# Attention on clusters and a gated feed-forward block: loads of one pair behind a transpose, logits later and in other banks, the last product stored in halves

## The chip, the cores and the metric

The kernel runs on one core of a Trainium2 chip. The metric is the device time of one execution in microseconds (us). The kernel before took 321.58 us (median of three runs, 321.5 to 322.22).

The core's engines run side by side and each works through its own instructions in order: TensorE (PE in the profile; its weight loads are PEld), VectorE (DVE), ScalarE (ACT), GpSimd (POOL) and SyncE (SP), which here issues nearly all DMAs. A DMA is issued by an engine and then carried out by the core's 16 DMA engines. Matrix products land in PSUM, which has eight banks; everything else lies in SBUF.

## The reference

Four batches, eight heads, 768 tokens, 64 numbers a head. Each query and key goes to the nearest of 16 centroids of its head; a query sees the keys of its own cluster alone. The attention's output, 512 numbers a token, goes through a gated feed-forward block with 1,536 inner columns.

```python
q_assign = argmax(einsum('bhsd,hcd->bhsc', q_n, c_n))      # and k_assign alike
mask = q_assign[:, :, :, None] == k_assign[:, :, None, :]
scores = where(mask, scale * q @ k.T, -1e9)
x = (softmax(scores) @ v).transpose(0, 2, 1, 3).reshape(B * S, H * D)
out = (sigmoid(x @ w_gate) * (x @ w_val)) @ w_out
```

## The kernel before

**Attention.** Heads go in pairs: batch b, pair p, head e of the pair (0 or 1). A step of the main loop is one score product `sc` (line 894): 128 keys against 384 queries of one head, an exponential on ScalarE (line 899), and, two steps later, three products `av` with the values (line 917). There are 96 steps a batch, 384 in all. Batch 1 begins with step 96, batch 2 with step 192, batch 3 with step 288; in them a pair's first use is 24 steps after the one before it (batch 2: steps 192, 216, 240, 264). The last pair of a batch is worked in two halves.

**Preparing a pair** (`pair_prep`, from line 1452) is done long before its first use, with these steps, each under a name:

- `ld`: SyncE loads k, q and v of the pair, 384 KB each (line 212), into three buffers a kind.
- `sp`: VectorE casts to 16 bits and GpSimd makes the remainder (lines 1459 and 1460), giving `hl`.
- `tn0`, `tn1`: SyncE transposes `hl` of head 0 and head 1 by DMA into `T` (`turn`, line 411).
- `lg0`, `lg1`: TensorE makes the logits of a head, 12 small products from `T` into one PSUM bank `lg` (`logits1`, line 435).
- `pk0`, `pk1`: VectorE reduces the logits, finds the maximum and writes the marks `oh` (lines 450, 461, 463, 470). The bank of `lg` is free after the first of these five operations.
- `ot`: SyncE transposes the marks by DMA (line 1477), and `hp0`, `hp1` copy them, four DMAs called hops, into rows of `T` (line 491). The pair's scores need them.
- `vc`, `vs`: casts and sums of v.

After the last step of a pair its outputs are normalised (lines 371 to 376) and SyncE transposes them into `xTb` (line 948), the input of the feed-forward block.

**Feed-forward.** A block of 384 tokens is cut in 12 times two pieces, `g` (line 531, tanh on ScalarE) and `v` (line 547, combined on VectorE into `hT`, line 552), and then output products. In batch 0 these are plain: an output tile `o` of 12 products in one bank (line 685), then a copy (lines 693 and 695). From batch 1 on they are factored in seven products over two output banks (line 822, additions on VectorE, line 769); between `begin` and `end2` the flag `taken["pair"]` says that a product holds both banks. The pieces go one by one between the steps, by a budget of nanoseconds a step (`ns...`). The last block is closed by `closing` (line 576), whose last product, `last`, is made in two halves of 128 columns, `o_end`.

**PSUM.** Four banks are a ring (`bank`, line 162) for scores, `g`, `v` and most other things; two hold `av`; two are output banks (`out_bank`, line 167). `turns` (line 171) takes an output bank, or one of the ring while `taken["pair"]` is set. A tile that takes a bank waits until the former tile of that bank has been read.

**Order.** Nothing is reordered by a tool: the order of the instructions on each engine is that in which the code issues them. `SCHED` says when: a key `b2ld` or `b2p1lg0` is a distance in steps from the pair's first use. The key without a pair (`b2...`) holds for batches 2 and 3, one with `b2p1` for pair 1 of batch 2 alone. The loads stand at first use + `b2ld` + an offset of their own for k, q and v (`b2p1lk` and so on). Within a step the order is: score, what is due at the half step, feed-forward pieces, `av`, what is due at the full step (`run_bg`). An issue on SyncE waits for its data, and what stands behind it waits too.

Of the kernel before, what the change touches and what calls it, by code (L numbers as in the profile page):

```python
# [8 lines left out]
FP = mybir.dt.float32  # L9
# [86 lines left out]
}  # L96


# [1 line left out]
def kernel(  # L100
# [12 lines left out]
    PE, ACT, DVE, POOL, SP = nc.tensor, nc.scalar, nc.vector, nc.gpsimd, nc.sync  # L113
    B, H, S, D = q.shape
    NCL = centroids.shape[1]
    DM = out.shape[1]
# [45 lines left out]
    def bank(n=512, dt=FP, name="bank"):  # L162
        return ring.tile([128, n], dt, tag="ring", name=name)
# [3 lines left out]
    def out_bank():  # L167
        taken["op"] += 1
        return op.tile([128, DM], FP, tag="o", name="o")
# [94 lines left out]
    HF, HD = NFC // 2, DM // 2  # L264
# [163 lines left out]
    def logits(t, h, n, copy=None):  # L428
        return logits1([(t, c, h) for c in range(n)], copy)

    def logits1(groups, copy=None):
        n = len(groups)
        lg = (turns if SCHED.get("lgo1", 0) else bank)(512, FP, name="lg")
        for i, (t, c, h) in enumerate(groups):
            PE.matmul(  # L435
                out=lg[:, bass.ts(i, 32)], lhsT=t[:, c, :],
                rhs=cm[:, h].rearrange("p s n -> p (s n)"), start=True, stop=True,
            )
        lv = lg[:, 0 : n * 32].rearrange("p (c s n) -> p c s n", s=2, n=NCL)
        if SCHED.get("lgr", 0) and (n > 6 or SCHED.get("lgs", 0)):  # L440
            return lv, None
        lo = smp.tile([128, 12, NCL], FP, name="lglo")
        (copy or ACT.copy)(lo[:, 0:n], lv[:, :, 1, :])
        return lv[:, :, 0, :], lo[:, 0:n]
# [53 lines left out]
    def tok(b, t, f):  # L498
        return HB[b, t // 3][:, HF * f : HF * f + HF, bass.ts(t % 3, 128)]

    def store(src, b, c0, n, m=slice(0, DM)):
        def f():
            SP.dma_start(
                out=out[b * S : (b + 1) * S].rearrange("(p c) m -> p c m", c=NCH)[
                    :, c0 : c0 + n, m
                ],
                in_=src,
            )

        d_ = SCHED.get("sd", 0)  # L510
        if d_ > 0 and b < B - 2:
            at(step_no[0] + d_, f)
        else:
            f()
# [61 lines left out]
    def closing(b, gv, ma, mb):  # L576

        ac, order = [], []  # L580
        plus = lambda dst, a, z: DVE.tensor_tensor(dst, a, z, ALU.add)

        def pair(m, bk):
            st = {}
            lhs = {
                1: lambda: tok(b, m.t1, 0), 2: lambda: tok(b, m.t1, 1), 4: lambda: tok(b, m.t2, 1),
                6: lambda: m.of[2], 5: lambda: m.of[1], 7: lambda: m.of[3], 3: lambda: m.of[4],
            }
            rhs = {1: B11, 2: B21, 3: B22, 4: T4, 5: T1, 6: T2, 7: T3}
            C = lambda i, j: st["ob"][:, i, HD * j : HD * j + HD]  # L590

            def mm(o, k, g, n, start, a=0, z=HD):
                w = lhs[k]()
                for c in range(g, g + n):
                    PE.matmul(  # L595
                        out=o, lhsT=w[:, c, :], rhs=rhs[k][:, c, a:z],
                        start=start and c == 0, stop=c == HF - 1, skip_group_check=True,
                    )

            def product(k, g=0, n=HF):  # L600
                def f():
                    z = {1: "a", 4: "d", 6: "x", 7: "x", 5: "y", 3: "y"}[k]
                    if g == 0 and k in (1, 4, 6, 5):
                        if k == 1:
                            st["ob"] = osp.tile([128, 2, DM], FP, name="ob")
                        st[z] = bk(z)
                    o = st[z][:, 0:HD]
                    mm(o, k, g, n, k not in (7, 3))
                    if g + n < HF:
                        return  # L610
                    if k == 1:
                        ACT.activation(C(0, 0), o, AF.Copy)
                    elif k == 4:
                        plus(C(1, 0), o, C(0, 0))
                    elif k == 6:
                        plus(C(0, 1), o, C(0, 0))
                    elif k == 5:
                        plus(C(1, 1), o, C(0, 0))
                    elif k == 7:
                        plus(C(1, 0), o, C(1, 0))  # L620
                        plus(C(1, 1), o, C(1, 1))
                        store(st["ob"][:, 1:2], b, m.t2, 1)
                    else:
                        plus(C(0, 1), o, C(0, 1))
                        store(st["ob"][:, 0:1, HD:DM], b, m.t1, 1, slice(HD, DM))

                return f

            def last(parts):
                def f():  # L630
                    for a, z in parts:
                        o = bank(z - a, name="o_end")
                        mm(o, 2, 0, HF, True, a, z)
                        plus(st["ob"][:, 0, a:z], o, st["ob"][:, 0, a:z])
                    store(st["ob"][:, 0:1, 0:HD], b, m.t1, 1, slice(0, HD))

                return f

            return product, last

        two = {}

        def bank_a(z):
            if z in "ad":
                need(*(("wo", i) for i in range(WOP)), *(("wt", i, c) for i in range(4) for c in range(2)))
                two[z] = out_bank()
            return two[{"x": "a", "y": "d"}.get(z, z)]

        pa, la = pair(ma, bank_a)
        pb, lb = pair(mb, lambda z: bank(512, name="o_end"))  # L650
        early = [pa(k, g, HF // 2) for k in (1, 4, 6, 5) for g in (0, HF // 2)]

        def drained(f):
            def g():
                while aside:
                    aside.pop(0)[1]()
                f()

            return g

        early[0] = drained(early[0])
        atoms = gv[:14]
        for i, x in enumerate(gv[14:]):
            atoms.append(x)
            if i < len(early):
                atoms.append((0.0, early[i]))
        for f in (
            pa(7), pb(1), pb(4), pa(3), pb(6), pb(5), la([(0, HD)]), pb(7), pb(3),
            lb([(0, HD // 2), (HD // 2, HD)]),
        ):  # L670
            atoms.append((0.0, f))
        return atoms
# [278 lines left out]
    step_no = [-4]  # L951

    def at(i, f):
        bg.setdefault(max(i, step_no[0] - 0.5), []).append(f)
# [11 lines left out]
    def need(*names):  # L966
        for n in names:
            assert n in done, n
# [133 lines left out]
    def first(p, e, parts=1):  # L1102
# [55 lines left out]
        def lg(part=0):  # L1158
            cs = [c for s in range(2 if part == 0 else 1) for c in range(*rng(s, part))]
            gs = [(T[0, h], c, h) for c in cs]  # L1160
            if SCHED.get(f"hL{h}", 0) and h:
                st["lg", part] = join(*logits1(gs, SCHED.get(f"hM{h}", 0) and DVE.tensor_copy))
            else:
                st["lg", part] = logits2(gs, h == 0 and part == 0)
# [65 lines left out]
    def rest(p, i):  # L1230
# [41 lines left out]
        def lg(eng=None):  # L1272
            gs = [(T[0, 2 * p + e], 6 + P0 + c, 2 * p + e) for e in range(2) for c in range(N)]
            st["lg"] = join(*logits1(gs)) if SCHED.get(f"rL{p}" + "_" * (i - 1), 0) else logits2(gs)
# [25 lines left out]
        def pl(e, eng=None):  # L1300
            if SCHED.get(RO, 0):
# [10 lines left out]
               lg=-15, pk=-14, ot=-10, pl0=-9, pl1=-7, oe=-9, hp=-8)  # L1312
# [17 lines left out]
    a = P[0, 0, 0]  # L1330
# [53 lines left out]
    def put(nm, key, u, off, f, arg):  # L1384
# [15 lines left out]
        def go():  # L1400
# [7 lines left out]
                 lg=-9, pk=-8, ot=-5, pl0=-4, pl1=-3)  # L1408
# [121 lines left out]
    for b in range(B):  # L1530
        xT = xtp.tile([128, NDC, S], HP, tag="xTb", name="xTb")
        key = min(b, 1)
        for i in range(2 if b else NPT):
# [4 lines left out]
            c0, cn = PARTS[i] if b == 0 else (3 * i, 3)  # L1538
            for w in range(1 + (cn > 3)):
                z = cn // (1 + (cn > 3))  # L1540
# [51 lines left out]
```

## Time and profile before

| | |
|---|---|
| median of three runs | 321.58 us |
| profiled execution, its own time | 323.41 us |
| its span, first to last instruction | 321.6 us |
| TensorE busy | 314.1 us (98%), 3510 matmuls |
| VectorE, ScalarE, GpSimd busy | 225.2, 230.8, 108.9 us |
| DMA | 45.16 MB, 140 GB/s over the span |
| the chain that ended last | TensorE 92%, VectorE 3%, DMA 2% |
| granted TensorE clock | 1.000 |

The profiled execution is one execution with the hardware profiler on; its times are microseconds from the span's start. A row of the order of time has start, length, engine, line, operation, what it writes and reads, sizes, and in brackets the idle time of the engine before it with what ended it. Matmuls are pipelined, and the profile's ends of matmuls are modelled: two that follow each other without a wait overlap. So a loss on TensorE is read from start to start where it is short. For a DMA the length is that of the issue on SyncE; the time from issue to landing is told by the view of DMA issues.

### The profile page before, as it was taken

Reading aid. Unit: us, or ns where it says so; the run is one execution under the profiler, and the core shown is the slowest. Engines: PE = TensorE matmul, PEld = TensorE weight load, DVE = VectorE, ACT = ScalarE, POOL = GpSimd, SP = SyncE. Lnnn points to the kernel's source line nnn. Section 1 sums busy time; section 2 is a strip of 40 time slices with the busy share of each in tenths; the row PEclk is TensorE's granted clock in tenths of the full one; section 3 lists DMA queues with packets and bytes.
Section 4 is the critical chain, followed back from the end, with each engine's and each line's share of the span. In section 5 each row is a group of like instructions: output and inputs, shape, how many; then the busy total and the mean of one; then the engine's idle time right before and its main releaser. Section 6 shows DMA issues by size and latency. Waiting matters only on the chain.

```text
span 321.6 us, 9181 instructions
## 1 busy us (share of the span) xinstructions
PE 314.1 (98%) x3510; PEld 222.1 (69%) x3510; DVE 225.2 (70%) x598; ACT 230.8 (72%) x521; POOL 108.9 (34%) x145
## 2 busy tenths in 40 slices
PE   7999999999999998999999999999999999999996
PEld 5888666766766665666777678666777678667775
DVE  5899656777787676686778678775766456456666
ACT  6688988787889986877767786887877875332320
POOL 6887464154435364423233342524102011000000
DMA  7999996748776996965665545952512122200103
GB/s 204 372 264 193 237 169 122 190 93 237 236 114 184 166 218 142 275 175 108 111 200 138 188 101 155 258 89 53 110 27 66 39 27 73 84 2 1 65 2 131
DMA packets 77708, 45.16 MB, mean 140 GB/s; under 512 B 56864, under 2 KB 75104, under 8 KB 77664
## 3 DMA queue, kind: packets, MB, share of 16 engines
q1 hardware_dynamic: 73696, 39.73, 49.4%
q0 software_dynamic: 3680, 4.72, 8.8%
q8 instruction: 27, 0.44, 0.6%
q14 instruction: 17, 0.14, 0.2%
q10 hardware_dynamic: 288, 0.13, 0.1%
HBM read 28.34 MB, written 6.29 MB: 108 GB/s over the span
## 4 chain that ended last, share of the span: by engine, by line
PE 92%; DVE 3%; DMA 2%; ACT 1%; issue 0%; ACTq 0%; POOL 0%; DVEq 0%
PE g L531 20%; PE v L547 19%; PE sc L894 18%; PE av L917 10%; PE o L822 10%; PE o L685 3%; DMA T<-hl 2%; PE lg L435 2%; PE o_end L595 2%; PE lg L422 1%; PE o L595 1%; PE oh_ps L1203 1%; PE t_ps L1143 1%; PE wm L985 1%; PE t_ps L1026 0%
## 5 line engine op out<-in xcount | busy, mean ns | idle before, releaser
L899 ACT ACTIVATE es<-sc 128x384 f16<-128x384 f32 x384 | 173.9, 492 | 40.5 <-PE sc L894 29.9
L894 PE MATMUL sc<-T 128*128 128x384 f16 x384 | 117.5, 326 | 0.4 <-DVE T L1224 0.4
L917 PEld LDWEIGHTS <-es 128*128 128x128 f16 x1152 | 81.3, 98 | 35.1 <-ACT es L899 0.2
L917 PE MATMUL av<-va,es 128*128 128x65 f16 x1152 | 97.6, 194 | 0.0
L552 DVE SCALAR_TENSOR_TENSOR hT<-th,v 128x384 f16<-128x384 f32 x96 | 53.1, 553 | 57.3 <-PE av L917 36.4
L531 PE MATMUL g<-xTb,wg 128*128 128x384 f16 x384 | 78.0, 326 | 0.2 <-DVE hT L552 0.2
L547 PE MATMUL v<-xTb,wv 128*128 128x384 f16 x384 | 78.1, 326 | 0.1
L537 ACT ACTIVATE th<-g 128x384 f32<-128x384 f32 x96 | 47.2, 492 | 34.7 <-PE g L531 15.6
L376 POOL TENSOR_TENSOR xp<-t,rec 128x384 f16<-128x384 f32 (+1 forms) x30 | 21.6, 721 | 98.0 <-DVE rec L373 50.3
L531 PEld LDWEIGHTS <-wg 128*128 128x128 f16 x384 | 37.3, 97 | 19.2 <-issue 0.4
L547 PEld LDWEIGHTS <-wv 128*128 128x128 f16 x384 | 37.4, 98 | 19.0 <-issue 0.3
L894 PEld LDWEIGHTS <-T 128*128 128x128 f16 x384 | 37.1, 97 | 0.6 <-DVE T L1224 0.5
L1460 POOL TENSOR_TENSOR hl<-kraw,hl 128x384 f16<-128x384 f32 x22 | 20.3, 922 | 41.4 <-DVE hl L1459 26.7
L1460 POOL TENSOR_TENSOR hl<-qraw,hl 128x384 f16<-128x384 f32 x22 | 21.2, 963 | 11.1 <-DVE hl L1459 11.1
L769 DVE TENSOR_TENSOR ob<-o,ob 128x256 f32<-128x256 f32 (+1 forms) x35 | 17.9, 523 | 6.9 <-PE o L822 4.1
L685 PE MATMUL o<-wo,hT 128*128 128x512 f16 x72 | 19.9, 379 | 0.0
L371 DVE TENSOR_TENSOR t<-av,sv 128x390 f32<-128x390 f32 (+1 forms) x30 | 14.4, 480 | 7.7 <-PE av L917 5.6
L822 PE MATMUL o<-wo,hT 128*128 128x256 f16 x126 | 19.7, 272 | 0.0
L822 PEld LDWEIGHTS <-sum 128*128 128x128 f16 x168 | 16.3, 97 | 4.4
L450 DVE TENSOR_REDUCE lgs<-lg 128x192 f32<-128x384 f32 x23 | 12.7, 551 | 3.7 <-PE lg L435 3.6
L822 PEld LDWEIGHTS <-hT 128*128 128x128 f16 x126 | 12.1, 97 | 3.3
L323 POOL CAST va<-vraw 128x768 f16<-128x768 f32 x15 | 13.0, 866 | 2.3 <-DMA vraw<-in_v_dram 2.3
(158 smaller groups left out, 340.0 us busy)
## 6 DMA issues: line engine op xcount, KB each, us to landing
vraw<-in_v_dram SPq DMA_DIRECT2D x15, 384.0 KB, 5.2
kraw<-in_k_dram SPq DMA_DIRECT2D x14, 384.0 KB, 4.4
qraw<-in_q_dram SPq DMA_DIRECT2D x12, 384.0 KB, 4.3
out_dram<-ob SPq DMA_DIRECT2D x18, 256.0 KB, 2.2
wg<-in_moe_w_gate_dram POOLq DMA_DIRECT2D x2, 768.0 KB, 9.2
wv<-in_moe_w_val_dram POOLq DMA_DIRECT2D x2, 768.0 KB, 10.2
wo<-in_moe_w_out_dram POOLq DMA_DIRECT2D x2, 768.0 KB, 9.0
T<-ohT SPq DMA_DIRECT2D x44, 24.0 KB, 1.9
```

The costliest lines, as they stand in the source:

```text
L376: (eng or POOL).tensor_tensor(x, t[:, 0:nq, 0:64], bcast(rec[:, 0:nq], 64), ALU.mult)
L531: PE.matmul(out=g[:, 0:n], lhsT=wg[fc // WQ][:, dc, fc % WQ, :], rhs=xT[:, dc, t0 : t0 + n], start=(dc == 0), stop=(dc == NDC - 1),)
L537: ACT.activation(th[:, 0:n], g[:, 0:n], AF.Tanh)
L547: PE.matmul(out=w[:, 0:n], lhsT=wv[fc // WQ][:, dc, fc % WQ, :], rhs=xT[:, dc, t0 : t0 + n], start=(dc == 0), stop=(dc == NDC - 1),)
L552: DVE.scalar_tensor_tensor(HB[b, blk][:, fc, 0:n], st[0][:, 0:n], 1.0, w[:, 0:n], ALU.add, ALU.mult)
L685: PE.matmul(out=o, lhsT=HB[b, blk][:, fc, bass.ts(t, 128)], rhs=wo[fc // WON][:, fc % WON, :], start=(fc == 0), stop=(fc == NFC - 1),)
L769: plus = lambda dst, a, z: DVE.tensor_tensor(dst, a, z, ALU.add)
L822: PE.matmul(out=st[z][:, e], lhsT=a[:, c, :], rhs=rhs[:, c, :], start=start and c + e == 0, stop=c == HF - 1, skip_group_check=True,)
L894: PE.matmul(out=sc.rearrange("p (c t) -> p c t", t=128), lhsT=s["k"], rhs=s["q"], start=True, stop=True,)
L899: ACT.activation(es, sc, AF.Exp, scale=SCALE)
L917: PE.matmul(out=av[:, a0 + s["c0"] + i, :], lhsT=s["es"][:, bass.ts(i, 128)], rhs=VA[b, p][:, e, s["j"], :], start=(first and i == 0 and a ...
L1460: POOL.tensor_tensor(hl[:, :, 64:128], r, hl[:, :, 0:64], ALU.subtract)
```

## The change

- `b2p2lk`, `b2p2lq`, `b2p2lv`: the loads of pair 2 of batch 2 move from steps 157, 157.5 and 158.5 to steps 168, 168 and 169. Pair 1's `tn0` stands at step 166.5. (The offsets are set for batch 2 alone; pair 3 of both batches and pair 1 of batch 2 had such offsets already.)
- `b2p1lg0`, `b2p1pk0`: batch 2, pair 1: the logits of head 0 move from step 177 to 180, their marks from step 177 to 180.5.
- `b2pk1`: in all pairs of batches 2 and 3 the marks of head 1 come one step earlier, half a step behind their logits.
- `logits1` takes its bank by `turns` from step 101 on, not from the ring.
- `store` takes an engine, and `last` stores each half of the last product behind its addition: the first half from SyncE, the second from ScalarE, where both went in one store from SyncE. The `last` of the other tile of that block, with one part, stores from SyncE as before.

```diff
-    "b2tn1": -39.5, "b2lg1": -29, "b2pk1": -27.5, "b2ot": -21.0, "b2hp0": -13.5, "b2hp1":
+    "b2tn1": -39.5, "b2lg1": -29, "b2pk1": -28.5, "b2ot": -21.0, "b2hp0": -13.5, "b2hp1":
...
-    "b3p0vs": -30, "b3p0vu": -28, "b3p0vt": -9, "b3p1lg0": -32, "b3p1pk0": -32, "END": 0,
+    "b3p0vs": -30, "b3p0vu": -28, "b3p0vt": -9, "b3p1lg0": -32, "b3p1pk0": -32, "b2p2lk": 10.5, "b2p2lq": 10.5, "b2p2lv": 11.5, "b2p1lg0": -36, "b2p1pk0": -35.5, "END": 0,
...
     def logits1(groups, copy=None):
         n = len(groups)
-        lg = (turns if SCHED.get("lgo1", 0) else bank)(512, FP, name="lg")
+        lg = (turns if step_no[0] > 100 else bank)(512, FP, name="lg")
...
-    def store(src, b, c0, n, m=slice(0, DM)):
+    def store(src, b, c0, n, m=slice(0, DM), eng=SP):
         def f():
-            SP.dma_start(
+            eng.dma_start(
...
             def last(parts):
                 def f():
-                    for a, z in parts:
+                    for i, (a, z) in enumerate(parts):
                         o = bank(z - a, name="o_end")
                         mm(o, 2, 0, HF, True, a, z)
                         plus(st["ob"][:, 0, a:z], o, st["ob"][:, 0, a:z])
-                    store(st["ob"][:, 0:1, 0:HD], b, m.t1, 1, slice(0, HD))
+                        store(st["ob"][:, 0:1, a:z], b, m.t1, 1, slice(a, z), (SP, ACT)[i])
```

## The prediction

> **What bounds the kernel now.** I read the page first, then the busy time of each engine in stretches, then the order of time around the holes.
>
> ```profile
> span 321.6 us, 9181 instructions
> ...
> core 0: us, PE busy (x) PEld busy (x) DVE busy (x) ACT busy (x) POOL busy (x), PEclk, DMA share, GB/s
> 40.00:120.00 80.00, 80.00 (x929) 53.29 (x928) 58.55 (x153) 69.42 (x160) 35.56 (x41) 1.00 0.78 173
> 120.00:123.00 3.00, 1.71 (x27) 1.04 (x24) 1.60 (x5) 1.08 (x3) 1.34 (x2) 1.00 1.12 150
> 123.00:218.00 95.00, 94.93 (x1050) 66.67 (x1049) 70.46 (x186) 73.81 (x166) 33.98 (x41) 1.00 0.67 160
> 218.00:220.00 2.00, 1.79 (x20) 1.07 (x18) 1.46 (x4) 1.19 (x4) 0.00 (x0) 1.00 0.50 114
> 220.00:318.60 98.60, 98.55 (x899) 70.16 (x897) 61.05 (x145) 53.61 (x118) 9.53 (x13) 1.00 0.19 48
> 318.60:321.60 3.00, 0.00 (x0) 0.00 (x0) 0.29 (x1) 0.00 (x0) 0.00 (x0) 1.00 0.48 175
> ```
>
> Each row of a stretch has its length and then the busy time of each engine. From 40 us on TensorE is never idle but in three places: 1.29 us in 120 to 123, 0.21 in 218 to 220, and the 3.0 us after its last matmul. The change adds or removes no matmul, so it can only win there, or lose by opening new holes. The granted clock is 1.00 throughout.
>
> ```profile
> 120.52 0.26 PE L917 MATMUL av<-va,es 128*128 128x65 f16 x3
> 122.06 0.47 PE L435 MATMUL lg<-cm,T 128*128 128x32 f16 x12 [1.29 <-DMA T<-hl]
> ...
> 217.00 0.26 PE L917 MATMUL av<-va,es 128*128 128x65 f16 x3
> 217.09 0.45 PE L435 MATMUL lg<-cm,T 128*128 128x32 f16 x12
> ```
>
> Idle time is measured from a modelled end. From start to start, the logits of 122.06 stand 1.54 us behind the products in front of them; those of 217.09, which wait for nothing, stand 0.09 behind theirs. So that stop costs 1.45. By the count of score matmuls it lies in step 177: it is `lg0` of batch 2's pair 1, one of the two entries that the change moves on their own.
>
> **Part 1: the loads of batch 2's pair 2 go behind pair 1's transpose, pair 1's `lg0` three steps later.** SyncE's issues in order of time (start, length of the issue), then from the view of DMA issues, by windows that hold one each, what four of them took from issue to landing (the first is that of 114.93, then 116.88, 122.14, 126.25):
>
> ```profile
> 112.21 0.58 SPq L212 DMA_DIRECT2D kraw<-in_k_dram  x1
> 112.84 0.46 SPq L212 DMA_DIRECT2D qraw<-in_q_dram  x1
> 114.06 0.37 SPq L212 DMA_DIRECT2D vraw<-in_v_dram  x1
> 114.93 1.86 SPq L411 DMA_TRANSPOSE T<-hl  x1
> 116.88 2.23 SPq L1477 DMA_TRANSPOSE ohT<-oh  x1
> ...
> 122.14 1.46 SPq L411 DMA_TRANSPOSE T<-hl  x1
> 123.71 2.50 SPq L491 DMA_DIRECT2D T<-ohT  x4
> 126.25 1.25 SPq L948 DMA_TRANSPOSE xTb<-xp  x1
> ...
> T<-hl SPq DMA_TRANSPOSE x1, 7.1
> ...
> ohT<-oh SPq DMA_TRANSPOSE x1, 5.7
> ...
> T<-hl SPq DMA_TRANSPOSE x1, 3.5
> ...
> xTb<-xp SPq DMA_TRANSPOSE x1, 2.4
> ...
> 114.00 0.91 POOL L1460 TENSOR_TENSOR hl<-qraw,hl 128x384 f16<-128x384 f32 x1
> ...
> DMA  8999999999200799999999999500000000799999
> q8 instruction: 1, 0.02, 1.3%
> ```
>
> The three loads of 112.21 to 114.06 are the ones moved (planned at steps 157 to 158.5, now 168 to 169). The transpose `tn0` of 114.93 (step 166.5) took 7.1 us behind them and landed at 114.93 + 7.1 = 122.0, just when the logits started; its twin of 122.14, with no loads ahead, took 3.5. Its source was ready at 114.00 + 0.91 = 114.9, so it is issued no earlier than now. Without the loads ahead it lands at 114.93 + 3.5 = 118.4. Step 177 without a stop comes at 120.6, so the landing alone removes the whole 1.45, and `lg0` at step 180 only adds margin (step 192's score stands at 129.68 below: 15 steps in 7.6 us, so 1.5 us for three). The moved loads keep their use: the first cast of that pair's k stands at 125.19, some 123.7 after the change; the issue goes to about 116.9, and behind a transpose, with the 5.7 us that one such took, it lands at 122.6.
>
> The last two rows show 117.0 to 122.5 in 40 slices of 0.1375 us: from 120.5 to 121.7 the DMA engines move nearly nothing, and one 16 KB block of instructions was fetched in this stretch. Some 1.1 us of the 7.1 are this hole. The Trainium skill (Runtime: NRT & Kernel Launch, "Instruction fetch mechanics") says that a 16 KiB refill is mostly hidden; by that rule the hole would be an accident of this execution, which is what rival B takes it for.
>
> What pays for it: `ohT` (116.88) now stands behind the three loads. Their issues take 0.58 + 0.46 + 0.37, with gaps about 1.6 us, so it is issued at 118.5; with the 5.7 us that it took behind the transpose it lands at 124.2 instead of 122.6. The four hops that read it were issued from 123.71 and go to 124.25; `xTb` behind them goes from 126.25 to 126.8. Who needs that:
>
> ```profile
> 129.68 0.33 PE L894 MATMUL sc<-T 128*128 128x384 f16 x1
> 129.84 0.33 PE L531 MATMUL g<-xTb,wg 128*128 128x384 f16 x1
> ...
> 124.41 0.38 PE L685 MATMUL o<-wo,hT 128*128 128x512 f16 x1
> ...
> 124.11 0.69 DVE L693 COPY ob<-o 128x512 f32<-128x512 f32 x1
> ```
>
> Batch 1's first `g` at 129.84 reads that `xTb`. 1.45 earlier it wants it at 128.4. SyncE's issues from 122.14 on stand back to back (each starts 0.04 to 0.1 after the one before ends) and don't move forward: landing 126.25 + 2.4 = 128.65 as it is, 129.2 with the late hops. So 0.25 to 0.8 of the 1.45 goes to this new wait; I take 0.45, nearer the end in which `ohT` lands a little late, since loads and hops overlap in part. The first hops are needed by the score at 129.68, then 128.2; issued at 124.25 they would have to take 4 us to be late.
>
> One more wait hides below it. The plain output that begins at 124.41 now finds the logits in one output bank and must take the bank whose copy runs until 124.11 + 0.69 = 124.80, 0.39 behind its own start. The moved logits, though, stand between the two outputs and take about 0.3 (12 matmuls, 0.45 with the last one's own length), so about 0.1 is left; it comes before `g` and counts inside the 0.45. Net of part 1: -1.45 + 0.45 = **-1.0** (bounds -1.2, and -0.1 in rival B).
>
> **Part 2: logits in the output banks.** From step 101 on `logits1` takes one of two output banks unless a factored product holds both. By the order of products in the trace it does so for 13 of 19 logits; the other six stay in the ring.
>
> ```profile
> 218.55 0.33 PE L894 MATMUL sc<-T 128*128 128x384 f16 x1
> 219.08 0.65 PE L531 MATMUL g<-xTb,wg 128*128 128x384 f16 x3 [0.20 <-DVE hT L552]
> ...
> 218.47 0.56 DVE L552 SCALAR_TENSOR_TENSOR hT<-th,v 128x384 f16<-128x384 f32 x1 [1.54 <-PE av L917]
> 218.94 0.55 DVE L450 TENSOR_REDUCE lgs<-lg 128x192 f32<-128x384 f32 x1
> ...
> 220.38 0.19 DVE L470 TENSOR_SCALAR oh<-oh 128x96 f16<-128x96 f16 x1
> ```
>
> The logits of 217.09 (step 307) hold a ring bank until their reduce ends at 218.94 + 0.55 = 219.49, so scores, `g` and `v` turn in three banks; `g` starts at 219.08, right behind the `hT` that frees one. It stands 0.53 behind the score before it (218.55), against 0.16 between score and `g` at 129.68 and 129.84: 0.37 lost, which a fourth bank gives back. Waits under 0.15 that busy time doesn't show may give as much again elsewhere. I take **-0.55** (bounds 0 and -0.8). The price is an output or product that begins before the reduce is done: the 0.1 above is one, and none can cost more than the reduce and what stands ahead of it on VectorE; with two banks, the one freed first is there for the next.
>
> **Part 3: `pk1` one step earlier**, in batches 2 and 3, eight times. It is the block from the reduce at 218.94 to 220.38 + 0.19 = 220.57, 1.63 us. VectorE stood idle 1.54 us before the `hT` of 218.47, waiting for TensorE. One step earlier the block falls into that idle time, and `hT` comes at most 0.6 later, with a fourth bank free meanwhile. I take 0 (bounds -0.2 and +3, rival C).
>
> **Part 4: the last product stored by halves.**
>
> ```profile
> out_dram<-ob SPq DMA_DIRECT2D x4, 128.0 KB, 1.7
> kraw<-in_k_dram SPq DMA_DIRECT2D x1, 96.0 KB, 2.1
> kraw<-in_k_dram ACTq DMA_DIRECT2D x1, 96.0 KB, 2.5
> ...
> DMA  0000003599799979979999999999995200000000
> ```
>
> The last row is 318.5 to 320.8: the DMA engines are full from about 318.9 to 320.2 with the stores queued before, so a first half issued sooner has no room, and both halves end with the same bytes. ScalarE's queue saves only an issue. Against it, the one pair of like loads took 0.4 longer there. I take **0** (bounds -0.15 and +0.8). The Trainium skill (DMA: Bandwidth & Descriptors, "Rules for kernel authors") calls transfers under 64 KB mostly overhead and asks to merge them; by that rule halves of 64 KB gain nothing and rival D is the likelier way, while the 1.7 us of 128 KB here shows no such limit yet.
>
> **Sum.** -1.0 - 0.55 + 0 + 0 = -1.55 us. The profiled execution took 323.41 around its span of 321.6; by the sum 321.9. The median of the runs is 321.58, 1.83 below the profiled one; I put the same sum on it: **320.0**.
>
> **Rivals.** A, the forecast: TensorE gets back most of the stop and the bank: 321.58 - 1.2 - 0.8 - 0.15 = 319.4 at best, 320.6 at worst.
>
> B, the stop isn't there in runs without the profiler, or SyncE's chain eats it: the hole of 1.1 us is part of the 1.45, so 0.35 is left to win, and the `xTb` bound takes 0.25 of that. With part 2, 321.58 - 0.1 - 0.55 = 320.9. For it: profiled and unprofiled differ by 1.83; against: the instruction block lies at a fixed place of the program. This also stands for a change that does nothing.
>
> C, slower: VectorE's early block. If at each of the eight places the later `hT` frees its bank too late and costs the 0.37 of 219.08, that is 8 x 0.37 = 3.0, and 321.58 - 1.55 + 3.0 = 323.0. It outweighs the gain from 0.2 per place on. For it: VectorE works in order and `g` already waited on `hT` once; against: its idle 1.54 in front.
>
> D, ScalarE's queue lands the last half 0.8 later (2.5 against 1.7): 320.0 + 0.8 = 320.8.
>
> **How the numbers follow.** 0.3% is 0.96 us, about what a measurement of this kernel tells from no change. A 0.60, B 0.21, D 0.06, C 0.13. Faster is A; same is B and D, 0.27; slower is C. The range takes A, B and D, 0.3 us below for the spread of the runs (321.5 to 322.22) and of C what costs up to 0.25 at each place (8 x 0.25 - 1.55 = 0.45): 319.1 to 322.0; A alone 319.4 to 320.6.
>
> **What would show it.** Right: `tn0` of that pair lands 3.5 to 4.2 us after its issue, TensorE has no wait on `T<-hl`, 120 to 123 is over 2.9 busy, the wait on `hT` near 218 is gone. Wrong: an idle row of over 0.8 at batch 1's first `g`, or a wait on `T<-hl` at a later step; many small waits `g <- hT`; a last store on ScalarE's queue of over 2.2 us.

## The result and the profile after

The changed kernel takes 324.38 us (median of five runs, 323.63 to 326.02) against 321.74 for the one before beside it (321.5 to 322.22): a ratio of 1.0078, 95% interval 1.0059 to 1.0097, some 2.5 us slower. The prediction was 320.0, with 319.1 to 322.0 as its range: wrong in sign.

The span of the changed kernel and its busy time by stretches; a row has the stretch, its length, then PE, PEld, DVE, ACT and POOL busy, granted clock, DMA share and GB/s.

```profile
span 323.6 us, 9188 instructions
...
40.00:120.00 80.00, 79.56 (x922) 53.08 (x921) 57.58 (x152) 69.03 (x159) 35.83 (x42) 1.00 0.75 160
120.00:123.00 3.00, 3.00 (x33) 1.80 (x31) 2.10 (x5) 2.67 (x7) 1.64 (x3) 1.00 1.05 355
123.00:218.00 95.00, 93.06 (x1032) 65.35 (x1031) 70.06 (x185) 71.55 (x161) 32.59 (x41) 1.00 0.72 165
218.00:220.00 2.00, 2.00 (x29) 1.40 (x28) 1.34 (x3) 1.70 (x4) 1.43 (x2) 1.00 0.02 4
220.00:320.00 100.00, 99.99 (x916) 71.19 (x913) 61.91 (x146) 54.64 (x121) 9.51 (x13) 1.00 0.20 49
320.00:323.60 3.60, 0.01 (x1) 0.00 (x0) 0.30 (x2) 0.00 (x0) 0.00 (x0) 1.00 0.42 146
```

Both holes of before are closed: 120 to 123 and 218 to 220 are full. In their place 1.94 us are idle in 123 to 218, which was full but for 0.07, and TensorE has ended by 320.0 while the span goes on for 3.6 us, 0.5 more than before. The logits' waits, and the rows of `lg0` and `lg1`, in the views of waits and of the order of time (the two numbers after the total are how often and the longest):

```profile
PE lg L435 <- DMA T<-hl: 2.4, 2, 1.9
```

```profile
123.46 0.46 PE L435 MATMUL lg<-cm,T 128*128 128x32 f16 x12
129.50 0.47 PE L435 MATMUL lg<-cm,T 128*128 128x32 f16 x12 [1.94 <-DMA T<-hl]
```

`lg0` of pair 1 at 123.46 (step 180) waits for nothing. The stop has gone ten steps on, to the logits of the pair's other head: `lg1` at step 187, which reads what `tn1` transposes. From start to start it costs 2.1 us. The other wait of the first row, 0.44 us at 100.55, is the idle time in the stretch of 40 to 120. It lies ahead of the moved loads and also comes with v's load alone moved (0.33) and with `pk1` alone (0.34), whose edits begin behind it, so it goes with the execution and not with the change. SyncE's issues around the stop of `lg1`, and what they took from issue to landing (the transposes of 116.15 and 123.71 and `ohT`, in windows that hold one each):

```profile
110.16 2.45 SPq L491 DMA_DIRECT2D T<-ohT  x4
116.15 1.42 SPq L411 DMA_TRANSPOSE T<-hl  x1
117.63 0.58 SPq L212 DMA_DIRECT2D kraw<-in_k_dram  x1
118.25 0.50 SPq L212 DMA_DIRECT2D qraw<-in_q_dram  x1
118.80 0.47 SPq L212 DMA_DIRECT2D vraw<-in_v_dram  x1
119.36 1.23 SPq L1477 DMA_TRANSPOSE ohT<-oh  x1
120.69 1.32 SPq L948 DMA_TRANSPOSE xTb<-xp  x1
122.11 1.50 SPq L503 DMA_DIRECT2D out_dram<-ob  x1
123.71 2.35 SPq L411 DMA_TRANSPOSE T<-hl  x1
```

```profile
T<-hl SPq DMA_TRANSPOSE x1, 3.2
...
T<-hl SPq DMA_TRANSPOSE x1, 5.7
...
ohT<-oh SPq DMA_TRANSPOSE x1, 6.6
```

`tn0` lands 3.2 us after its issue, as the prediction wanted. But SyncE's queue now issues nothing from 110.16 + 2.45 = 112.6 to 116.15, where before it issued the three loads at 112.21 to 114.06, and all that stands behind `tn0` is crowded: `tn1` is issued 7.56 us behind `tn0` (7.21 before) and takes 5.7 instead of 3.5. It lands at 129.4, and the logits start at 129.50.

### The profile page after: what moved, and what is told of

It is laid out like the page before. It is cut to its first block, busy times and chain, and to the rows that moved or that the text cites. A ratio compares the mean times of both kernels' runs of the same rounds, so it can differ in the third digit from the quotient of the medians.

```text
span 323.6 us, 9188 instructions
## 1 busy us (share of the span) xinstructions
PE 314.3 (97%) x3510; PEld 222.2 (69%) x3510; DVE 225.3 (70%) x598; ACT 230.7 (71%) x521; POOL 108.7 (34%) x145
## 4 chain that ended last, share of the span: by engine, by line
PE 87%; DMA 5%; DVE 3%; POOL 1%; SPq 1%; issue 1%; ACT 0%; DVEq 0%
PE v L547 19%; PE g L531 19%; PE sc L894 17%; PE o L822 10%; PE av L917 10%; PE o L685 4%; DMA T<-hl 3%; PE lg L435 2%; DMA kraw<-in_k_dram 2%; PE o_end L595 2%; PE o L595 1%; POOL hl L1122 1%; PE lg L422 1%; PE oh_ps L1203 1%; PE t_ps L1143 1%
```

## The experiments

The first theory: the moved loads make `tn1` late and cost nearly all. Rivals: the logits in the output banks, VectorE's earlier block, or the stores at the end. All kernels are the one before with the edit named, unless they say otherwise. Each stands beside runs of the kernel before; in us, the ratio's excess is taken of 322.

| kernel | ratio to before | interval | us |
|---|---|---|---|
| before again | 0.9997 | 0.9985 to 1.0010 | -0.1 |
| three loads moved | 1.0056 | 1.0036 to 1.0076 | +1.8 |
| changed kernel without the loads' move | 0.9997 | 0.9984 to 1.0010 | -0.1 |
| split store alone | 1.0041 | 1.0027 to 1.0055 | +1.3 |
| output banks alone | 0.9982 | 0.9970 to 0.9995 | -0.6 |
| `pk1` alone | 0.9987 | 0.9973 to 1.0001 | -0.4 |
| banks, `pk1`, `lg0` | 0.9977 | 0.9966 to 0.9988 | -0.7 |
| loads moved, `lg1` later | 1.0032 | 1.0020 to 1.0045 | +1.0 |
| v's load moved | 0.9996 | 0.9986 to 1.0006 | -0.1 |
| k's and q's loads moved | 1.0051 | 1.0031 to 1.0072 | +1.6 |
| `lg0` and `pk0` alone | 0.9995 | 0.9986 to 1.0004 | -0.2 |
| changed kernel, one last store | 1.0045 | 1.0027 to 1.0062 | +1.4 |
| stores split, count as before | 1.0031 | 1.0019 to 1.0042 | +1.0 |
| banks, `pk1`, stores split, count as before | 0.9984 | 0.9963 to 1.0006 | -0.5 |

**The kernel before, run again.** No edit.

> The kernel before once more, unchanged, to see what belongs to an execution and what to the program. If the wait of 1.45 us at step 177 and the 40 us of the lead-in are the program's, both come back within 0.3 us and the time is within 0.3% of the kernel before. If they are an accident of the one profiled execution, the wait is under 0.5 us here.

Logits and transposes of pair 1 in order of time, then the landing of the transposes:

```profile
120.66 0.46 PE L435 MATMUL lg<-cm,T 128*128 128x32 f16 x12
...
126.20 0.47 PE L435 MATMUL lg<-cm,T 128*128 128x32 f16 x12
```

```profile
114.97 1.44 SPq L411 DMA_TRANSPOSE T<-hl  x1
...
121.77 1.46 SPq L411 DMA_TRANSPOSE T<-hl  x1
```

```profile
T<-hl SPq DMA_TRANSPOSE x1, 5.3
...
T<-hl SPq DMA_TRANSPOSE x1, 4.4
```

The 1.45 us stop that the prediction wanted to win is not there: `tn0` lands at 114.97 + 5.3 = 120.3, just ahead of the logits. And `tn1` lands at 121.77 + 4.4 = 126.2, just as its logits start (they lose 0.12 from start to start). So `tn1` has no slack here. In the profile that the prediction read it had 1.8 us (landing at 122.14 + 3.5 = 125.6, logits at 127.50), but only because the stop at step 177 had put everything off.

**The loads alone, and the rest without them.**

```diff
-    ... "END": 0,
+    ... "b2p2lk": 10.5, "b2p2lq": 10.5, "b2p2lv": 11.5, "END": 0,
```

> The kernel before with only the three loads of batch 2's pair 2 moved to steps 168, 168 and 169. Theory (the loads now crowd the transpose for the logits of step 187): the wait at step 177 goes (-1.45), a wait of about 2 us comes at step 187: 0.3 to 0.9 us slower than before. Rival (the loss is in the lead-in and at the end, not here): 1 to 1.5 us faster than before, no wait over 0.5 at step 187.

> The changed kernel with the three loads left where they were; all else of the change stays. Theory: no wait at step 187 and, with the logits three steps later, none over 0.2 at step 180: 1 to 2 us faster than before, 3 to 4 faster than the changed kernel. Rival: the changed kernel's time within 1 us, so still slower than before.

```profile
128.44 0.47 PE L435 MATMUL lg<-cm,T 128*128 128x32 f16 x12 [1.83 <-DMA T<-hl]
```

The row is that of `lg1` with the loads alone moved: the same stop, 2.0 us from start to start, and +1.8 us in the time. That is more than the 0.3 to 0.9 expected, since there was no 1.45 to win back. Without the move the other parts together are level with before, and not 1 to 2 us faster as expected. The loads carry the loss.

**Which of the loads: v's alone, then k's and q's.**

```diff
+    "b2p2lv": 11.5,                     (v's alone)
+    "b2p2lk": 10.5, "b2p2lq": 10.5,     (k's and q's)
```

> Before, with only v's load of the three moved behind the transpose tn0 (k's and q's stay in front of it). Theory (a queue served in order, with no slack at pair 1's second transpose tn1, which in the repeat of before landed 0.04 us ahead of the logits that read it): each load moved behind tn0 pushes tn1 about a third of what three did (they made it 2.0 us late), so the logits at step 187 wait 0.6 to 1.0 us on T<-hl, and the time goes up by 0.4 to 0.9 us. Rival 1 (it is the pause in the transfers around an instruction fetch that makes tn1 late, whatever stands ahead): a stop of 1.5 to 2.1 there as with three loads, +1.4 us or more. Rival 2 (there is slack for one load): no stop over 0.2, time within 0.3 us of before.

> Before, with k's and q's loads moved behind the transpose tn0 and v's left in front of it (v's load alone behind tn0 cost nothing; all three cost 1.8 us). Theory (SyncE's queue stands idle between k's and q's early issue and tn0, so their bytes were moved for nothing there; v's buffer comes free only 0.9 us before tn0's issue, so its bytes fall into tn0's time on either side): nearly the whole loss is k's and q's, tn1 lands 12.6 us or more after tn0's issue (11.2 in the repeat of before and with v alone moved, 13.1 with all three), the stop at step 187 is 1.5 to 2.1, and the time is 1.1 to 1.8 us above before. Rival (every load counts the same beyond the first, which is free): a stop of 0.8 to 1.3 and 0.4 to 0.9 us.

With v's load behind `tn0`: issues, the landing of `tn1`, and its logits.

```profile
112.40 0.46 SPq L212 DMA_DIRECT2D qraw<-in_q_dram  x1
115.37 1.43 SPq L411 DMA_TRANSPOSE T<-hl  x1
116.85 0.57 SPq L212 DMA_DIRECT2D vraw<-in_v_dram  x1
...
120.84 2.29 SPq L411 DMA_TRANSPOSE T<-hl  x1
```

```profile
T<-hl SPq DMA_TRANSPOSE x1, 5.9
```

```profile
126.79 0.47 PE L435 MATMUL lg<-cm,T 128*128 128x32 f16 x12
```

With k's and q's behind it:

```profile
114.12 0.40 SPq L212 DMA_DIRECT2D vraw<-in_v_dram  x1
114.99 2.14 SPq L411 DMA_TRANSPOSE T<-hl  x1
117.18 0.57 SPq L212 DMA_DIRECT2D kraw<-in_k_dram  x1
...
122.57 2.27 SPq L411 DMA_TRANSPOSE T<-hl  x1
```

```profile
128.29 0.47 PE L435 MATMUL lg<-cm,T 128*128 128x32 f16 x12 [2.03 <-DMA T<-hl]
128.61 0.32 PE L894 MATMUL sc<-T 128*128 128x384 f16 x1
...
129.51 0.51 PE L894 MATMUL sc<-T 128*128 128x384 f16 x1
```

From the issue of `tn0` to the landing of `tn1` it is 11.2 us in the kernel before run again (114.97 to 126.2), 11.4 with v's load moved (115.37 to 120.84 + 5.9) and 13.3 with k's and q's (114.99 to 128.29, where the logits start). With all three, in the changed kernel, it is 13.3 too (116.15 to 129.4): against the repeat `tn1` is issued 0.8 us later behind `tn0` (7.56 against 6.80) and takes 1.3 longer (5.7 against 4.4). My first expectation, a third of the loss for a third of the loads, fell: v's load costs its logits 0.3 from start to start (0.12 in the repeat) and nothing in the time, and the two others cost nearly everything. The pause of the DMA engines told of at the end of this text does not make the difference: it lies between the issue of `tn0` and the landing of `tn1` in all four profiles. The second expectation held: the idle stretch of the queue fits all of this. k's and q's loads were issued there, at 112.2 to 113.3; without them, in the changed kernel, the DMA engines move nothing from 113.7 to 117.1. v's is not issued before 114.1, since its buffer waits for GpSimd's cast of the v before it (line 323), so its bytes fall into the transposes' time on either side of `tn0`. One load of k or q alone was not moved, so that it is the stretch and not the number of bytes rests on v's load adding nothing, alone or on top of the two.

The last two rows show a second price of such a stop. Up to 128.61 a score takes 0.32 us, at 129.51 it takes 0.51: the granted clock is 0.51 in 129 to 132, and by step 193 the scores have lost another 1.65 us against the repeat. This profiled execution is the slowest of its twelve (325.9 us). Four of the twelve have a mean granted clock of 0.993 or 0.994 and take 324.57 us or more; the median of the other eight is 323.1, some 1.1 above before. After the stops of the other profiles (1.94 idle in the changed kernel, 1.83 with the loads alone, 2.40 with one last store) the clock stays at 1.00 and nothing more is lost. What decides it was not tried.

**Later logits for `tn1` too.** The loads moved, and `lg1` of that pair from step 187 to 191, its block to 191.5.

```diff
+    "b2p2lk": 10.5, "b2p2lq": 10.5, "b2p2lv": 11.5, "b2p1lg1": -25, "b2p1pk1": -24.5,
```

> The kernel before with the three loads moved as in the change, and head 1's logits of pair 1 four steps later (step 191, marks 191.5), so that the transpose that came late there has 2 us more. Theory (SyncE's whole chain behind the loads is late, and the input of batch 1's first g is its last link): the wait of 2 us moves to that g or to the score of step 192 and is still 1 to 2 us; time 0.8 to 1.8 us slower than before. Rival (only that one transpose is late): no wait over 0.4 there, time within 0.5 us of before.

```profile
128.15 0.47 PE L435 MATMUL lg<-cm,T 128*128 128x32 f16 x12
...
129.69 0.32 PE L531 MATMUL g<-xTb,wg 128*128 128x384 f16 x1 [0.24 <-DMA xTb<-xp]
```

The stop at the logits shrinks to 0.2 (128.15, which is 0.29 behind the products in front of it against 0.09) and the next reader of the queue stops: batch 1's first `g` on `xTb`, 0.41 from start to start, the very wait to which the prediction gave 0.45. Another 0.16 goes between these logits and the next score (0.48 from start to start against 0.32 in the repeat), for a reason that the trace does not name. Together that is 0.8 of the +1.0. So neither expectation came: there is no wait of 1 to 2 us, and the loss is not over with the one transpose either.

**The stop at step 177 by itself.** Only `lg0` and `pk0` at step 180.

```diff
+    "b2p1lg0": -36, "b2p1pk0": -35.5,
```

> Before, with only pair 1's first logits and their block at step 180 (the half of part 1 that has no price on the queue). In three of six executions of the old order the logits at step 177 stopped 0.9 to 1.7 us, in three not at all. Theory (a stop there is made up for at step 187, whose transpose lands at the same time either way, so nothing is left to win): time within 0.4 us of before, no stop at step 180, a stop of 0 to 0.2 at step 187. Rival (the stop was worth its 1.45 in the runs where it comes, about half of them): 0.5 to 0.9 us faster.

No stop is left at steps 177 to 187 in this trace, and the time does not move: -0.2, interval -0.5 to +0.1. In the seven executions with the loads in front and `lg0` at step 177, `tn0` landed late in three (the profile before, `pk1` alone, stores split with the count as before), with stops of 1.45, 1.7 and 0.9. In the other four it landed in time (the expectation left out one of these). The expected reason, that the stop is made up for at step 187, is not what the traces show. The scores of the profile before and of the repeat stand level up to step 176; then the stop puts the former 1.4 behind, and it is still 1.3 behind at the last score. So the stop costs nearly its length in the execution that has it: the profiled execution before took 323.41 us, 1.83 above the median of the runs beside it, and the two others with a stop, 322.98 and 323.94 us, are the slowest of twelve runs each. The median gains nothing from taking it away, so by that most executions do not have it; how often it comes without the profiler is not on record.

**Banks and block.**

```diff
-        lg = (turns if SCHED.get("lgo1", 0) else bank)(512, FP, name="lg")
+        lg = (turns if step_no[0] > 100 else bank)(512, FP, name="lg")
```

```diff
-    "b2pk1": -27.5,
+    "b2pk1": -28.5,
```

> The kernel before with only the logits' bank taken by turns from step 101 on. Theory (the fourth ring bank removes the short stops on g and v at about 184 and 218, some 0.37 + 0.23 + 0.2, and costs none): 0.5 to 0.9 us faster than before, no stop of over 0.15 on TensorE between 130 and 310. Rival (an output or product waits for the bank): a new stop of 0.3 or more, same time as before.

> The kernel before with only the marks of head 1 one step earlier in batches 2 and 3. Theory (VectorE's block falls into its idle time): within 0.3 us of before; the stop near 218 goes or stays below 0.4. Rival C of the prediction (a later combination frees its ring bank too late): new stops of 0.2 to 0.4 at several of the eight places, 1 to 3 us slower.

> The changed kernel without the moved loads and without the split store: banks by turns, marks of head 1 earlier, head 0's logits of that pair at step 180. By the runs so far (without the loads level with before, the split store alone 1.3 us slower): 0.8 to 1.5 us faster than before. Rival (the split costs little in this program, its end was 3.5 us behind the last matmul against 3.1): 0.3 to 0.6 us faster.

The stretch around step 307, in the kernel before run again, with the output banks, and with `pk1` earlier:

```profile
215.00:219.00 4.00, 3.80 (x46) 2.42 (x43) 2.39 (x7) 3.08 (x7) 1.30 (x2) 1.00 0.34 77
```

```profile
215.00:219.00 4.00, 4.00 (x51) 2.77 (x50) 2.36 (x9) 3.17 (x8) 0.91 (x1) 1.00 0.43 98
```

```profile
215.00:219.00 4.00, 4.00 (x52) 2.70 (x50) 2.81 (x9) 3.17 (x8) 1.83 (x2) 1.00 0.00 0
```

Each of the two edits alone takes away the wait `g <- hT`, which was worth 0.36 from start to start, so they cannot add fully: -0.6 and -0.4 alone, -0.7 together with `lg0`. That last kernel is faster than before, 321.54 against 322.05, by less than the 0.8 to 1.5 expected; that it is faster than the output banks alone (321.46) is not shown.

**The stores at the end.** The split alone, then the changed kernel with one last store:

```diff
-                    store(st["ob"][:, 0:1, 0:HD], b, m.t1, 1, slice(0, HD))
+                        store(st["ob"][:, 0:1, a:z], b, m.t1, 1, slice(a, z), (SP, ACT)[i])
```

> The kernel before with only the last product stored by halves, the second from ScalarE. Theory (the waits at the very end go through the DMA semaphores in a fixed order, some 0.06 us each, and one more DMA puts the last landing at their head instead of their end): the last landing comes no later after the last addition (1.8 us), but the end 0.4 us later, so 0.3 to 0.6 us slower than before. Rival (ScalarE's queue is the slower one): the landing itself comes 0.4 us later. Third case: no difference.

> The changed kernel with its last product stored in one piece as in before; all else as changed. If the parts add, loads +1.8, bank -0.6, block -0.4: 0.8 us above before, with the 2 us stop at step 187 still there and the end 3.1 us behind the last matmul. If part 4 costs what the closing waits show in the changed kernel (0.45), the time is 0.3 to 0.6 below that of the changed kernel. If instead the sum of the parts misses something that the later logits of step 180 cost, it stays 1.5 us or more above before.

With one last store the changed kernel is +1.4 against the runs of before beside it, where with two it was +2.5 against its own. It ends 3.1 behind its last matmul and keeps the stop of `lg1` (2.40 idle). So part 4 adds to the loss and the loads still make most of it. The end of the changed kernel, and its last two stores from issue to landing:

```profile
319.18 0.83 PE L595 MATMUL o_end<-wo,hT 128*128 128x128 f16 x12
319.51 1.30 SPq L503 DMA_DIRECT2D out_dram<-ob  x3
320.43 0.37 ACTq L503 DMA_DIRECT2D out_dram<-ob  x1
```

```profile
out_dram<-ob SPq DMA_DIRECT2D x1, 64.0 KB, 1.8
out_dram<-ob ACTq DMA_DIRECT2D x1, 64.0 KB, 1.6
```

The two halves start together, since SyncE is still busy issuing the store before. They land at 322.2 and 322.0, 2.2 us behind the last matmul, as the one store did before (318.96 + 1.8, with the last matmul ending at 318.56). Yet the span ends 1.34 behind the last landing, against 0.91 before. The compiled program tells why. SyncE's last instructions wait for eight DMA counters in a fixed order, and DMAs take the counters in turn:

```
SP EventSemaphore DMAHW0 >= 368
SP EventSemaphore DMAHW1 >= 352
...
SP EventSemaphore DMAHW7 >= 352
```

Before, the last store counts on the last of them. One store more puts SyncE's half, the last to land, on the first, and seven waits of some 0.06 us each follow it: in the trace of the changed kernel the first of the eight ends its wait at 322.24 and the last at 322.67. The next kernels keep the split but merge the part that is ready first with the store ahead of it, so that the count is as before (`split` is true for the block's second tile alone):

```diff
-            lb([(0, HD // 2), (HD // 2, HD)]),
+            lb([(HD // 2, HD), (0, HD // 2)]),
...
-                        store(st["ob"][:, 0:1, HD:DM], b, m.t1, 1, slice(HD, DM))
+                        if not split:
+                            store(st["ob"][:, 0:1, HD:DM], b, m.t1, 1, slice(HD, DM))
...
+                        e = DM if split and i == 0 else z
+                        store(st["ob"][:, 0:1, a:e], b, m.t1, 1, slice(a, e), (SP, ACT)[i])
```

> Before, with the last product stored in two parts again, but with the number of stores as in before: the store of the other column half is taken together with the part that is finished first (128x384 in one transfer on SyncE's queue), and the last part (128x128) goes on ScalarE's. Theory (the end is late in the changed kernel because SyncE's closing waits take the DMA counters in a fixed order, and one store more puts the last landing on the counter that is waited for first, with seven waits behind it): the last counter is the last again, the span ends 2.9 to 3.2 us behind the last matmul, and the time is within 0.4 us of before. Rival (smaller stores on two queues cost it by themselves): 3.4 us or more behind the last matmul and 0.4 to 1.3 us slower.

> Before with the two parts that paid (logits in the output banks, the block one step earlier), the loads where they were, and the last product in two stores with the count of stores unchanged. Theory: 0.6 + 0.4 us faster by the first two parts and 0 to 0.2 by the stores, some 321.0 us against 322.1 of before, the end 2.9 to 3.2 us behind the last matmul. Rival (smaller stores cost by themselves): no faster than 321.5 us.

The DMA view of the last stores, in the first of these kernels and in the second, which also has the output banks and `pk1`:

```profile
q14 instruction: 1, 0.01, 1.2%
...
out_dram<-ob SPq DMA_DIRECT2D x1, 192.0 KB, 1.9
out_dram<-ob ACTq DMA_DIRECT2D x1, 64.0 KB, 2.3
```

```profile
out_dram<-ob SPq DMA_DIRECT2D x1, 192.0 KB, 1.9
out_dram<-ob ACTq DMA_DIRECT2D x1, 64.0 KB, 1.8
```

In both, the span ends 0.91 behind the last landing again, so the order of the closing waits is the 0.43. But the first of them ends 3.96 behind the last matmul, not 3.07, and takes +1.0 us, the numbers of the rival: its last store was issued 0.3 later and took 0.6 longer to land, with an 8 KB block of instructions fetched among the stores (the first row). The split alone has such a fetch at 318.46, between its last issues and landings, and ends 4.44 behind the last matmul; no other profile here has one between the last matmul's end and the last landing, and the second kernel above, whose code differs only ahead of it, ends at 3.07. Of the 1.37 by which the split alone ends later, 0.27 lie behind the last landing (1.18 against 0.91) and 1.1 ahead of it, and these go with where that block is fetched. That the fetch is the cause I did not try by itself. The second kernel, of which some 321.0 us were expected, takes 321.54 against 322.16, with an interval that reaches over 1: the split gains nothing that these runs show.

## Why the prediction was wrong

**Part 1, "What pays for it", is the step that failed.** It followed `ohT`, the hops and `xTb`, which stand behind the moved loads, and asked who needs them. `tn1` stands behind the loads in the same queue, and the step left it at its 3.5 us. It took 5.7, was issued 0.8 later behind `tn0` than in the repeat, and its logits lost 2.1. The sentence "The moved loads keep their use" was right for the casts and no answer to what the idle stretch of the queue had been worth. The sum has nothing for it; the loads alone cost +1.8.

**Part 1, the gain.** That `tn0` lands soon after its issue without loads ahead came as said (3.2 us, 3.5 forecast), and no wait is left at `lg0`. But the -1.45 was read from an execution in which `tn0` fell behind the pause of the DMA engines. Others miss it by a fraction of a microsecond, and taking the stop away alone is worth 0.2 (-0.5 to +0.1). The step that failed here is "I put the same sum on it": the profiled execution was 1.83 above the median of the runs and 1.3 of that was the stop, so the gain was taken off a median that did not hold it. Rival B's premise was right and had 0.21.

**The wait on `xTb`**, 0.45 in the sum, is real (0.41 where `lg1` is moved on) and hidden behind the larger stop in the changed kernel. So is the wait of 0.1 put on the plain output behind the moved logits: in the changed kernel the output at 124.31 starts 0.30 behind its score instead of 0.16.

**Part 2** held, in the mechanism too: -0.55 predicted, -0.6 measured (-1.0 to -0.2), and step by step against the repeat the scores win 0.36 at the wait that was read and 0.36 at three smaller ones. **Part 3**: 0 predicted, -0.4 measured (-0.9 to 0); rival C's many small waits `g <- hT` are not there, and the edit removes one, which the sum did not have.

**Part 4** was mis-sized: 0 predicted with +0.8 as its bound, +0.45 behind the last landing in the changed kernel's trace, +1.3 alone. Rival D's reason was not it: ScalarE's half landed 1.6 us after its issue, sooner than SyncE's. The step "both halves end with the same bytes" was right as to the landing and left out what SyncE does after it. The Trainium skill (DMA: Bandwidth & Descriptors, "Rules for kernel authors") counts transfers under 64 KB as mostly overhead. The halves here are 64 KB each, at that size and not under it; in the changed kernel they landed 2.2 us behind the last matmul, as one store of 128 KB did, so there it is not their size that costs.

**The parts** by themselves sum to 1.8 - 0.6 - 0.4 + 1.3 = 2.1 of the 2.5 measured. With the split at its 0.45 in this program it is 1.3, and the changed kernel with one last store at +1.4 lies above the 0.8 that the other three give; the intervals (each about 0.5 to either side) allow it, and I cannot say whether the parts meet somewhere.

## What to carry to other kernels

Before a transfer is moved behind another, list everything that stands behind the new place in the same queue, with its slack, and ask whether the old place was an idle stretch of that queue: here the bytes of two loads cost nothing there, and elsewhere the transpose behind them paid. A stop in one profile lends slack to all that follows it, so slack is read from an execution without the stop, and a stop of this kind is looked for in a second profile before its whole length is counted as a gain. A profiled execution that is well above the median of the runs is a hint of one. An added DMA at the end also changes which counter is waited for last.

## What the runs showed of the hardware that was not expected

In the stretch of each of these profiles that holds the 16 KB instruction block, the DMA engines nearly stop for about a microsecond or more. The changed kernel from 120 to 127.5 us, in 40 slices of 0.1875, and its instruction fetch:

```profile
DMA  9889999999999999999900000019999999999999
...
q8 instruction: 1, 0.02, 1.3%
```

The pause is six slices, 1.1 us, from 123.75 on, in the middle of a queue that is otherwise full, and `tn1` (issued 123.71) sits in it. In the seven executions with the loads in front and `lg0` at step 177, `tn0` lands either ahead of it, at 119.7 to 120.3, or behind it, at 121.7 to 122.1. The Trainium skill (Runtime: NRT & Kernel Launch, "Instruction fetch mechanics") calls such refills mostly hidden. On TensorE's path here nothing is seen of this one in four of the seven executions, and in three it goes with a stop of 0.9 to 1.7 us. Whether the fetch causes the pause or only comes with it was not tried.

The issue itself varies by as much: `tn1` held SyncE for 1.46 us before and 2.35 after, `ohT` for 2.23 before and 1.23 after. What sets it was not tried.

The granted clock fell to half behind one stop of 2.03 us on TensorE, for 3.4 us, and cost 1.65 us more; behind three stops of 1.83 to 2.40 us in other executions it did not.
